# Moving the weight loads and weight casts of a fused convolution and token-mixer kernel onto the GpSimd queue, with a new job order

## The chip, the cores and the metric

The kernel runs on one core of a Trainium2 chip. The metric is the device time of one execution in microseconds (us), given as the median of several executions. "Span" is the time from the first to the last instruction of one profiled execution; the profiled execution of the kernel before took 160.67 us, 2.1 us longer than its span. Engines: TensorE (PE), VectorE (DVE), ScalarE (ACT), GpSimd (POOL), and the sync queue (SP), which only issues transfers.

## The reference

For each of 8 batches, x has 4224 rows of 192 columns. A causal convolution of 7 taps, one filter for each of 8 heads of 24 columns, gives y. Then a token mixer without a softmax follows:

```python
out = np.einsum('hk,bskhg->bshg', softmax(w), x_unf)      # y: 7-tap causal convolution
wq, wk = y @ w_q, y @ w_k                                 # 192 -> 64
W_tok = scale * np.einsum('bsd,btd->bst', wq, wk)
mixed = np.einsum('bst,btd->bsd', W_tok, y)
return np.maximum(mixed, 0.0) @ w_out
```

The kernel uses that mixed = wq (wk^T y) scale, and wk^T y = w_k^T (y^T y). So each batch needs y^T y once (the Gram matmuls), a small product M, and then Z = wq M, a ReLU and the output product.

## The kernel before

The convolution is a matmul with a band matrix (jobs Y); its result is evacuated to SBUF as `y`. The Gram matmuls (jobs G) want 64 of the 192 columns of y a second time beside the others, so a **duplicate copy** (job D, 128 x 1152 elements for half a batch) is made by DVE for batches 0 and 1 and by POOL for later ones. Then come Q (y with w_q), the small products for M, Z, and O (the output product). A small scheduler in the kernel file simulates all engines, gives each job a priority (`KEYS`), and so fixes each engine's instruction order at build time.

POOL issues the loads of x, which cast f32 to bf16 on the way (their queue, q0, counts 13.63 MB written, and the page has 27.73 MB read from HBM).

```python
    def load(b, part):                      # issued by POOL
        if b < NX and b not in zero:        # NX = 5 buffers for x
            zero[b] = [pool(lambda e: e.memset(XW[0:6, b, 0, 0, :], 0.0)),
                       pool(lambda e: e.memset(XW[:, b, :, NCK - 1, :], 0.0))]
        ...
        if part == 0:
            first(b, xg[b][0], old)                  # two small loads around the halo
            rows(b, 0, 1, 0, 128, 8, xg[b][0], old)
            rows(b, 1, 0, 0, 128, 9, xg[b][0], old)
        else:
            rows(b, 0, 9, 0, 128, 8, xg[b][1], old)
            rows(b, 1, 9, 0, 128, 8, xg[b][1], old)
            last(b, xg[b][1], old)
    ...
    for b in range(2, NX):                  # all ahead of the first duplicate
        load(b, 0)
        load(b, 1)
    ...
    def prefetch(b, part):                  # later loads, after a duplicate
        if b < B:
            load(b, part)
    ...
            if what == "dup":
                if key[1] > 1:              # batches 2 to 7
                    eng = "pool"
                    begin[eng] = max(free[eng], at)
    ...
        if kind == "D" and job.name[1] > 0:
            prefetch(job.name[1] + NX - 1, job.name[2])
```

The weights wk and wo come by the sync queue in f32, and ten small jobs on ACT and DVE cast them:

```python
        job_w("wk", 0, WK[:, 0], twice(WST[:, 0, 0:DH]), 128, 1),
        ...
        job_w("wo", 3, WO2S[:, :], WST[:, 3, :], D, 2),
```

Of the kernel before, what the change touches and what calls it, by code (L numbers as in the profile page):

```python
# [13 lines left out]
KEYS = {  # L14
    "E": -2.342, "Y": (-1.064, 1.033, 0.024), "Q": (-0.288, 1.999, -0.374), "G": (0.16, 0.5, 0.0),
    "Z": (0.931, 0.953, 0.0), "O": (1.4, 0.82, 0.0),
}

EDGES = {}


CLOCK = {
    "x0": (6.0, 8.2, 8.6, 9.8, 11.9, 13.7, 15.5, 16.5), "band": 6.7, "wq": 7.2, "wk": 15.0,
    "wo": 18.5, "now": 0.05, "hold": 1.5, "fill": 24.0, "issue": 3.0,
    "dma": (377e3, 14.5, 1.6, {"x": 3.0, "o": 1.2}),
# [138 lines left out]
def bass_lightweight_conv__then__hypermixer_token_mlp_kernel(  # L164
# [34 lines left out]
    def sbuf(name, shape, dtype):  # L199
# [18 lines left out]
    BANDL = sbuf("bandl", [128, H, 128], BF16)  # L218
    IDENT = sbuf("ident", [128, 128], BF16)
    WST = sbuf("wst", [128, 4, D], F32)  # L220
# [15 lines left out]
    WARM = sbuf("warm", [128, 128], BF16)  # L236
# [6 lines left out]
    THREES = ((0, 1, 2), (3, 4, 5), (6, 7))  # L243
    GROUPS = [[
        ((0,), 1, 6, FOURS), ((1,), 0, 5, FOURS), ((0,), 0, 1, (FOURS[0] + FOURS[1],)),
        ((0,), 6, 11, FOURS), ((1,), 5, 10, FOURS), ((0,), 11, 18, THREES), ((1,), 10, 14, FOURS),
        ((1,), 14, 18, FOURS),
    ]] + [[((0, 1), 0, 9, PAIRS), ((0, 1), 9, 18, PAIRS)]] * (B - 1)
# [46 lines left out]
    )  # L295
    for i in range(4):
        P.dma(
            "sp",
            lambda e, i=i: e.dma_start(
                WSQ[32 * i : 32 * i + 32, :, :].rearrange("p (m r) d -> p m (r d)", m=3),  # L300
                bass.AP(wq_t, 0, [[2 * DH, 32], [64 * DH, 3], [1, 2 * DH]]),
            ),
            wl[0],
        )
# [7 lines left out]
    z_m = dve(lambda e: e.memset(M_SB[:, :, :], 0.0))  # L312
    z_bandl = act(lambda e: e.memzero(BANDL[:, :, :]))  # L313
    z_ones = act(lambda e: e.activation(ONES[:, :], WARM[0:H, :], AF.Identity, bias=1.0), [z_warm])

    rows(0, 0, 1, 0, 128, 5, xg[0][0], ())
    bits = pool(lambda e: e.iota(BITS[:, :], [[1, H]], base=127, channel_multiplier=-1))
    rows(0, 1, 0, 0, 128, 5, xg[0][1], ())
    first(0, xg[0][2], z_first)
    rows(0, 0, 6, 0, 128, 5, xg[0][3], ())  # L320
# [7 lines left out]
    def wload(slot, p0, p1, src, row0, width, grp, deps, col=0):  # L328
        P.dma(
            "sp",  # L330
            lambda e: e.dma_start(
                WST[p0:p1, slot, col : col + width],
                bass.AP(src, row0 * width, [[width, p1 - p0], [1, width]]),
            ),
            grp, deps,
        )

    for s, (src, wd) in enumerate(((wk_t, DH), (wo_t, D))):
        wload(2 * s, 0, 128, src, 0, wd, wl[s + 1], [xg[0][2 * s]])
        if s == 0:  # L340
            wload(1, 0, 128, src, 64, wd, wl[1], ())
            wload(0, 0, 64, src, 128, wd, wl[1], (), DH)
            wload(0, 64, 128, src, 0, wd, wl[1], (), DH)
        else:
            wload(3, 0, 64, src, 128, wd, wl[2], ())
            wload(3, 64, 128, src, 128, wd, wl[2], ())


    def warm(n, deps):
        def f(e):  # L350
            for _ in range(n):
                o = e.matmul(PS[:, 0, 0:128], WARM[:, :], WARM[:, :], start=True, stop=True)
            return o

        return P.op("pe", f, deps)

    warm(16, [z_warm])
# [20 lines left out]
    zero = {}  # L378
    for b in range(1, NX):
        if b < 3:  # L380
            zero[b] = [act(lambda e, b=b: e.memzero(XW[0:6, b, 0, 0, :])),
                       act(lambda e, b=b: e.memzero(XW[:, b, :, NCK - 1, :]))]
    z_wk = act(lambda e: e.memzero(WK[:, 3:6]))
    z_wo2 = act(lambda e: e.memzero(WO2[:, :]))
# [37 lines left out]
    for q, eng in enumerate(("act", "dve", "act", "dve")):  # L422
# [3 lines left out]
        def f(e, q=q, x0=x0, x1=x1, s0=s0, eng=eng):  # L426
# [6 lines left out]
    wqs = [act(lambda e: e.copy(WQ[:, :, :], WSQ[:, :, :]), [wl[0]])]  # L433

    short = [dve(lambda e: e.tensor_copy(BANDL[0:64, :, 0:LAST], BAND[0:64, :, 0:LAST]),
                 [*band, z_bandl])]

    def load(b, part):
        if b < NX and b not in zero:
            zero[b] = [pool(lambda e: e.memset(XW[0:6, b, 0, 0, :], 0.0)),  # L440
                       pool(lambda e: e.memset(XW[:, b, :, NCK - 1, :], 0.0))]
        old = zero[b] if b < NX else [
            done[("Y", b - NX, g, k)] for g, q in enumerate(GROUPS[b - NX]) for k in range(len(q[3]))
        ]
        if part == 0:
            first(b, xg[b][0], old)
            rows(b, 0, 1, 0, 128, 8, xg[b][0], old)
            rows(b, 1, 0, 0, 128, 9, xg[b][0], old)
        else:
            rows(b, 0, 9, 0, 128, 8, xg[b][1], old)  # L450
            rows(b, 1, 9, 0, 128, 8, xg[b][1], old)
            last(b, xg[b][1], old)

    load(1, 0)
    load(1, 1)
    ident = pool(lambda e: e.memset(IDENT[:, :], 0.0))
# [6 lines left out]
    )  # L463
    z_zr = pool(lambda e: e.memset(ZR[:, :, 1, :], 0.0))
    for b in range(2, NX):
        load(b, 0)
        load(b, 1)
    warm(20, [])


    class Job:
        def __init__(self, name, key, banks, pe, cols, reads=(), after=(), evacs=(), then=None,
# [4 lines left out]
            self.pe_us = sum(max(n, 64) / 2400 + 0.0025 for n in cols)  # L477

    made = {"short": short, "band": band, "ident": [ident], "wq": wqs, "z_m": [z_m], "z_zr": [z_zr]}
# [13 lines left out]
    def parts(c0, c1):  # L493
        if c1 < NCK:
            return [(BAND, c0, c1)]
        return [(BAND, c0, c1 - 1), (BANDL, c1 - 1, c1)]

    def bands(c1):
        return ["band", "short"][: 1 + (c1 == NCK)]

    def job_y1(b, g, k):
# [3 lines left out]
        w = GRP * n  # L505

        def pe(e, bk):
            for j, h in enumerate(hs):
                for band_, a0, a1 in parts(c0, c1):
                    rhs = XW[:, b % NX, half, a0:a1, GRP * h : GRP * h + GRP]  # L510
                    o = PS[:, bk, w * j + GRP * (a0 - c0) : w * j + GRP * (a1 - c0)]
                    last = e.matmul(o, band_[:, h, :], rhs, start=True, stop=True,  # L512
                                    skip_group_check=True)
            return last

        def make(bk):
            o = bass.AP(
                Y, (b % 2) * NCK * 2 * YW + c0 * 2 * YW + YW * half + GRP * hs[0],
                [[2 * NCK * 2 * YW, 128], [GRP, len(hs)], [2 * YW, n], [1, GRP]],
            )  # L520
            i = PS[:, bk, 0 : w * len(hs)].rearrange("p (h c d) -> p h c d", c=n, d=GRP)
            return [(o, i)]

        return Job(
            ("Y", b, g, k), ykey(b, c0 + n * k / len(heads)), 1, pe,
            [GRP * (a1 - a0) for _, a0, a1 in parts(c0, c1)] * len(hs),
            reads=bands(c1), groups=[xg[b][g]],
# [3 lines left out]
    def job_y(b, g, hp):  # L531
# [5 lines left out]
        def pe(e, k):  # L537
            for j in range(2):
                h = 2 * hp + j
                for band_, a0, a1 in parts(c0, c1):  # L540
                    rhs = XW[:, b % NX, :, a0:a1, GRP * h : GRP * h + GRP]
                    o = PS[:, k + j, 48 * (a0 - c0) : 48 * (a1 - c0)]
                    last = e.matmul(  # L543
                        o.rearrange("p (c h d) -> p h c d", h=2, d=GRP), band_[:, h, :], rhs,
                        start=True, stop=True, skip_group_check=True,
                    )
            return last

        def make(k):
# [8 lines left out]
            ("Y", b, g, hp), ykey(b, c0 + n * hp / 4), 2, pe,  # L558
            [48 * (a1 - a0) for _, a0, a1 in parts(c0, c1)] * 2,
            reads=bands(c1), groups=[xg[b][g]],  # L560
            after=[("TD", b - 2, k) for k in range(6)] + [("G", b - 2, c) for c in range(NCK)],
            evacs=[(make, ("Y", b, g, hp), 96 * n, "copy")],
        )
# [68 lines left out]
    def job_g(b, c):  # L632
        def pe(e, bk):
            for h in range(2):
                y = Y[:, b % 2, c, h, :]
# [35 lines left out]
    def job_mm(b):  # L671
        def pe(e, bk):
# [10 lines left out]
            reads=[("wk", k) for k in range(6)] + ["z_m", ("GS", b), ("GT", b)],  # L683
# [56 lines left out]
    def job_o(b, i, q):  # L740
# [35 lines left out]
        def then():  # L776
# [21 lines left out]
            def landed(t, st=st):  # L798
                st.end = t

# [8 lines left out]
            reads=[("wo", k) for k in range(4)] + [("Z", b, i, k) for k in range(1 if rem else 3)],  # L809
# [4 lines left out]
    def twice(ap):  # L814
        return ap.unsqueeze(1).to_broadcast([ap.shape[0], 2, DH])

    def job_w(name, k, o, i, n, l, deps=()):
        return Job(
            ("W", name, k), KEYS["E"] + 0.01 * k, 0, None, [], reads=list(deps), groups=[wl[l]],
            evacs=[(lambda bk: [(o, i)], (name, k), n, "cast")],  # L820
        )

    made["z_wk"], made["z_wo2"] = [z_wk], [z_wo2]
    casts = [
        job_w("wk", 0, WK[:, 0], twice(WST[:, 0, 0:DH]), 128, 1),
        job_w("wk", 1, WK[:, 1], twice(WST[:, 1, 0:DH]), 128, 1),
        job_w("wk", 2, WK[:, 2], twice(WST[:, 0, DH : 2 * DH]), 128, 1),
        job_w("wk", 3, WK[0:64, 3], twice(WST[0:64, 0, 0:DH]), 128, 1, ["z_wk"]),
        job_w("wk", 4, WK[64:128, 4], twice(WST[64:128, 0, 0:DH]), 128, 1, ["z_wk"]),
        job_w("wk", 5, WK[64:128, 5], twice(WST[64:128, 1, 0:DH]), 128, 1, ["z_wk"]),  # L830
# [285 lines left out]
```

## Time and profile before

| | before |
|---|---|
| time, median of 3 | 161.17 us |
| span, granted clock | 158.6 us, 0.995 |
| busy PE, ACT, DVE, POOL | 91%, 81%, 74%, 39% |
| first output matmul | 31.21 us |
| end of the last matmul (its end is modelled) | 152.2 us |

### The profile page before, as it was taken

The page shows a single profiled execution, that of the slowest core. Times are in us where ns is not written, and L with a number is a line of the kernel's source. Part 1 is how long each engine was busy: PE and PEld are TensorE (multiplying, and loading weights), DVE is VectorE, ACT ScalarE, POOL GpSimd, SP SyncE. Part 2 cuts the span into 40 slices and gives each one's busy share as a digit, 9 for nine tenths or more (in the row PEclk, how much of TensorE's full clock was granted, in tenths as well). Part 3 has the DMA queues.
Part 4 walks back from the last instruction along what each step waited for, and adds up shares of the span by engine and source line. Part 5 has one row for each costly group of instructions (what it writes and reads, how often), then busy time and mean ns, then how long its engine had stood idle before and what let it go on. Part 6 is the DMA issues. An engine that isn't in the chain of part 4 may idle for free.

```text
span 158.6 us, 5869 instructions
## 1 busy us (share of the span) xinstructions
PE 144.7 (91%) x2553; PEld 110.3 (70%) x2584; DVE 117.3 (74%) x233; ACT 128.9 (81%) x225; POOL 62.0 (39%) x83
## 2 busy tenths in 40 slices
PE   5899968999998999999999999999999999999930
PEld 4899753777776667766776787687767777876720
DVE  6767757998748788869778887997679739556700
ACT  8633838999877999899799887978798989799960
POOL 7999999899990855022002020202011020000000
PEclk9999999999999999999999999999999999999997
DMA  2999999999999999999999999999996554679997
GB/s 44 187 179 205 191 191 192 191 190 268 213 258 310 300 200 283 330 256 298 288 296 286 297 290 243 278 336 295 251 346 235 199 207 189 236 269 371 360 386 256
DMA packets 48281, 40.44 MB, mean 255 GB/s; under 512 B 38144, under 2 KB 40320, under 8 KB 48256
## 3 DMA queue, kind: packets, MB, share of 16 engines
q0 software_dynamic: 36784, 13.63, 72.2%
q1 hardware_dynamic: 11472, 26.45, 46.2%
q8 instruction: 20, 0.33, 0.8%
q14 instruction: 5, 0.04, 0.1%
HBM read 27.73 MB, written 25.95 MB: 339 GB/s over the span
## 4 chain that ended last, share of the span: by engine, by line
PE 80%; ACT 8%; DVE 5%; issue 3%; ACTq 0%
PE ps L637 17%; PE ps L756 13%; PE ps L543 12%; PE ps L758 12%; PE ps L608 9%; PE ps L713 9%; ACT y L955 3%; PE ps L512 2%; PE ps L966 2%; ACT o_sb L955 1%; DVE yb L953 1%; PE ps L677 1%; DVE shift L415 1%; ACT L313 1%; ACT qt L955 1%
## 5 line engine op out<-in xcount | busy, mean ns | idle before, releaser
L955 ACT COPY o_sb<-ps 128x768 f32<-128x768 f32 (+1 forms) x63 | 47.2, 778 | 4.6 <-PE ps L758 3.4
L955 ACT CAST y<-ps 128x864 bf16<-128x864 f32 (+4 forms) x52 | 41.0, 814 | 6.7 <-PE ps L512 5.4
L756 PE MATMUL ps<-wo,zt 128*128 128x192 bf16 x256 | 42.6, 248 | 0.4 <-DVE m_sb L961 0.2
L758 PE MATMUL ps<-wo,zt 128*128 128x384 bf16 x128 | 41.7, 326 | 0.0
L268 POOL DMA_DIRECT2D xw<-in_x_dram x51 | 40.8, 820 | 1.5 <-POOLq L1101 0.8
L955 POOL COPY y<-y 128x1152 bf16<-128x1152 bf16 x12 | 13.9, 1155 | 66.6 <-ACT y L955 52.9
L637 PEld LDWEIGHTS ps<-y 128*128 128x128 bf16 x864 | 32.5, 98 | 8.5 <-ACT y L955 0.8
L637 PE MATMUL ps<-y 128*128 128x64 bf16 x864 | 35.8, 193 | 1.5 <-ACT y L955 0.4
L959 DVE TENSOR_SCALAR zt<-ps 128x512 bf16<-128x512 f32 x47 | 31.2, 683 | 7.8 <-PE ps L713 5.7
L953 DVE STREAM_TRANSPOSE yb<-y 128x576 int32<-128x576 int32 x48 | 33.6, 748 | 0.4 <-ACT y L955 0.2
L756 PEld LDWEIGHTS ps<-wo,zt 128*128 128x128 bf16 x256 | 25.6, 115 | 9.4 <-ACT o_sb L955 1.3
L543 PE MATMUL ps<-xw,band 128*128 128x432 bf16 (+1 forms) x112 | 28.5, 336 | 0.7 <-ACT m_sb L960 0.3
L958 ACT ACTIVATE zt<-ps 128x512 bf16<-128x512 f32 x49 | 28.8, 635 | 0.0
L955 DVE CAST y<-ps 128x864 bf16<-128x864 f32 (+2 forms) x20 | 19.3, 964 | 8.3 <-PE ps L543 5.4
L713 PE MATMUL ps<-qt,m_sb 128*128 128x512 bf16 x65 | 21.8, 380 | 0.3
L955 ACT CAST qt<-ps 128x576 bf16<-128x576 f32 (+2 forms) x21 | 11.7, 583 | 8.4 <-PE ps L608 8.4
L608 PE MATMUL ps<-yb,wq 32*64 32x288 bf16 x768 | 15.7, 284 | 0.9 <-issue 0.4
L955 DVE CAST qt<-ps 128x234 bf16<-128x234 f32 (+1 forms) x27 | 10.3, 419 | 8.2 <-PE ps L608 8.2
L543 PEld LDWEIGHTS ps<-xw,band 128*128 128x128 bf16 x112 | 9.8, 97 | 7.2 <-ACT m_sb L960 0.7
L758 PEld LDWEIGHTS ps<-wo,zt 128*128 128x128 bf16 x128 | 14.5, 113 | 0.0
L713 PEld LDWEIGHTS ps<-qt,m_sb 128*128 128x128 bf16 x96 | 8.8, 97 | 5.6 <-ACT y L955 0.9
L608 PEld LDWEIGHTS ps<-yb,wq 32*64 32x64 bf16 x768 | 10.5, 102 | 2.4 <-issue 1.3
(78 smaller groups left out, 118.9 us busy)
## 6 DMA issues: line engine op xcount, KB each, us to landing
out_dram<-o_sb SPq DMA_DIRECT2D x31, 768.0 KB, 7.3
xw<-in_x_dram POOLq DMA_DIRECT2D x21, 384.0 KB, 26.8
xw<-in_x_dram POOLq DMA_DIRECT2D x7, 432.0 KB, 26.1
xw<-in_x_dram POOLq DMA_DIRECT2D x4, 240.0 KB, 5.2
out_dram<-o_sb SPq DMA_DIRECT2D x16, 48.0 KB, 5.7
out_dram<-o_sb SPq DMA_DIRECT2D x2, 384.0 KB, 3.2
xw<-in_x_dram POOLq DMA_DIRECT2D x8, 42.0 KB, 13.4
xw<-in_x_dram POOLq DMA_DIRECT2D x1, 288.0 KB, 6.1
```

The lines of the kernel that those rows point to most:

```text
L268: return e.dma_start(XW[lo:hi, b % NX, half, c : c + n, :], bass.AP(x_t, at, [[D, hi - lo], [CW * D, n], [1, D]]),)
L512: last = e.matmul(o, band_[:, h, :], rhs, start=True, stop=True, skip_group_check=True)
L543: last = e.matmul(o.rearrange("p (c h d) -> p h c d", h=2, d=GRP), band_[:, h, :], rhs, start=True, stop=True, skip_group_check=True,)
L608: last = e.matmul(PS[64 * h : 64 * h + 64, bk + i, 0:288], WQ[r, j, :], rhs, start=j == 0, stop=j == 5, skip_group_check=True)
L637: last = e.matmul(PS[:, 7, 64 * k : 64 * k + 64], y[:, 64 * k : 64 * k + 128], y[:, 64 * k : 64 * k + 64], start=c + h + k == 0, stop=c == ...
L713: return e.matmul(PS[:, bk, :], m[:, parts[k] : parts[k] + 128], q, start=True, stop=True)
L756: e.matmul(o[:, 192 * h : 192 * h + 192], z[:, h, cols], WO1[:, :], start=h == 0, stop=False, **kw)
L758: last = e.matmul(o[:, 0:384], z[:, 2, cols], WO2[:, :], start=False, stop=True, **kw)
L953: return e.transpose(o, i)
L955: return e.copy(o, i) if eng == "act" else e.tensor_copy(o, i)
L958: return e.activation(o, i, AF.Relu)
L959: return e.tensor_scalar(o, i, 0.0, None, op0=ALU.max)
```

## The change

The intent was to shorten the start and to take small work off the busy engines. Batch 0's first two groups of x come by the sync queue in f32 and are cast on ACT and DVE; the halo rows of later batches are zeroed on DVE and not loaded apart; the last, short chunk uses the same band matrix; batch 0's band jobs may fill two PSUM banks; the weights are cast in their load, which POOL then issues; dummy matmuls that keep TensorE busy at the start are longer and fewer; the job priorities are new. The core of the diff:

```diff
-            first(b, xg[b][0], old)
-            rows(b, 0, 1, 0, 128, 8, xg[b][0], old)
-            rows(b, 1, 0, 0, 128, 9, xg[b][0], old)
+            for half in range(2):
+                rows(b, half, 9 * part, 0, 128, 9 - part, xg[b][part], old)
...
     load(1, 0)
+    wload(WK[:, 0], wk_t, 0, DH, wl[1], 2)            # on POOL, cast on the way
+    wload(WK[:, 1], wk_t, 64, DH, wl[1], 2)
+    wload(WK[0:64, 2], wk_t, 128, DH, wl[1], 2)
+    wload(WK[64:128, 2], wk_t, 0, DH, wl[1], 2)
+    wq = [pool(lambda e: e.tensor_copy(WQ[:, :, :], WSQ[:, :, :]), [wl[0]])]
     load(1, 1)
+    z_m = pool(...)      # and z_wk
+    load(1, 2)
+    wk = [pool(lambda e, o=o, i=i: e.tensor_copy(o, i), [wl[1]]) ...]     # 3 copies
+    load(1, 3)
+    wload(WO1[:, :], wo_t, 0, D, wl[2])               # and two more
+    load(2, 0)
+    z_wo2 = pool(...)
+    load(2, 1)
+    wo = [pool(lambda e, o=o, i=i: e.tensor_copy(o, i), [wl[2]]) ...]     # 2 copies
-    for b in range(2, NX):
+    for b in range(3, NX):
         load(b, 0)
         load(b, 1)
...
 KEYS = {
-    "E": -2.342, "Y": (-1.064, 1.033, 0.024), ...
+    "E": -4.9, "Y": (-1.039, 1.337, 0.0), ...         # new everywhere, and EDGES by batch
-                o = e.matmul(PS[:, k, 0:128], WARM[:, :], WARM[:, :], ...)
+                o = e.matmul(PS[:, k, 0:256], WARM[:, 0:128], WARM[:, 0:256], ...)
```

## The prediction

> **What bounds the kernel now.** I first read the engine shares of the page (TensorE 91% busy, the highest), then the chain of waits in order of time, then the busy time by stretch, then the DMA part.
>
> The chain gives the start-up and the real pace of TensorE, since its entries run from start to start:
>
> ```profile
> 6.59 0.98 PE ps L512 x8
> 7.57 1.39 PE ps L966 x13
> ...
> 9.97 0.81 PE ps L966 x12
> 10.99 0.87 PE ps L637 x30
> 12.08 0.56 PE ps L966 x10
> ...
> 19.69 0.35 ACT wo L955
> 20.04 0.25 ACT wo2s L955
> ...
> 21.60 1.03 issue
> 22.62 0.55 PE ps L966 x7
> ...
> 26.64 1.65 PE ps L713 x6
> 28.29 0.35 PE ps L637 x12
> ...
> 102.17 0.43 PE ps L713 x2
> ```
>
> Columns: start, length, what. The L966 pieces are dummy matmuls that only bridge idle time. L637 (the Gram jobs) takes 0.35/12 = 29 ns a matmul, L713 0.43/2 = 215 ns. The same view gives 90 ns per 216-column band matmul (0.36 for two of 432 columns), about 0.9 us per group of 48 in the Q job, and 0.33 us per output bank (0.17 for two of 192 columns, 0.16 for one of 384). Each is close to columns/2400 us + 2.7 ns. Over all jobs of the program that is 131 us of real TensorE work, without dummies. TensorE works from 6.59 to 152.0 us, so 14.5 us are lost, and they are not spread evenly:
> - up to the first output matmul (31.21 us in the timeline): 24.6 us hold 14.8 us of work. **9.8 us lost.**
> - from there to 152.0: 120.8 us hold 116.1 us. **4.7 us lost**, 4%.
> - after TensorE's end, 6.6 us of last evacuations and stores to the span's end at 158.6.
>
> So the start is worth attacking; the middle is nearly full. The stretches show the second resource (columns as in the page: the stretch, its length, busy time of PE, PEld, DVE, ACT, POOL, then granted clock, DMA share, GB/s):
>
> ```profile
> 24.00:34.00 10.00, 9.48 (x144) 6.13 (x146) 9.00 (x16) 9.81 (x16) 9.53 (x14) 1.00 1.60 192
> 60.00:80.00 20.00, 19.63 (x397) 14.78 (x409) 16.59 (x34) 18.02 (x30) 3.77 (x4) 1.00 1.28 295
> 120.00:130.00 10.00, 9.57 (x218) 7.65 (x221) 7.43 (x15) 8.91 (x18) 0.35 (x1) 1.00 0.56 213
> ```
> ```profile
> q0 software_dynamic: 36784, 13.63, 72.2%
> q1 hardware_dynamic: 11472, 26.45, 46.2%
> q8 instruction: 20, 0.33, 0.8%
> ```
>
> Queue q0 is the load of x, counted as written in bf16; in f32 it reads twice that, 27.3 MB. So 192 GB/s before the stores begin is 0.38 MB/us of reading, and 60 to 80 us (1.65 MB by q0, 4.2 by q1 in that window) is (3.3 + 4.2)/20 = 0.375 MB/us. Loads and stores together, 53 MB, need about 142 us of DMA: nearly the whole span. DMA has slack only after the last load landed (about 118 us, where q0 runs dry) and the share falls to 0.56. The DMA is a near second bound.
>
> [...]
>
> **The change part by part.**
> 1. *Input of batch 0.* Two of POOL's ten issues (820 ns each) move to the idle sync queue as plain f32 loads into unused output buffers, so the later groups are issued 1.6 us earlier. Before, TensorE still waits for the x DMA of group 6 at 16.3 us; the change's own timing table puts the last group at 13.7 instead of 16.5. Added: two casts of 128x960, one on ScalarE ahead of the band copies. From the 480- and 864-column casts (559, 903 ns) I estimate 1.0 us; if its data land by 4.8 us the band is not late by more than 0.2 us.
> 2. *Halo.* Per later batch two small loads go and one 6x96 memset comes (138 ns on DVE), saving 2 x 0.8 us of POOL issue, which is hidden after 40 us. Little.
> 3. *Last chunk.* The second band matrix goes: 72 band matmuls and 72 weight loads less, 0.8 us of TensorE, 0.45 of it after the first output. The Gram matmul contracts over 44 rows but streams as many columns: nothing.
> 4. *Two-bank jobs.* One 1.0 us evacuation for two of 0.56 and 0.66: about 0.2 us of evacuator time each, but 0.4 us more latency. Neutral.
> 5. *Weights cast in their load.* Ten small casts leave ScalarE and DVE between 15 and 21 us; the two lines of the chain above (0.60 us) and the cast at 16.23 (0.29) go. Added to POOL: 7 issues of about 0.7 us, and small copies, between the loads of batch 1. POOL is full until 34 us, but each issue of 9 chunks feeds 2.3 us of DMA.
> 6. *Dummies.* In the instruction order 83 fillers of 128 columns become 11 of 256, and 36 warm-up ones become 10 long ones. Filler on the chain is 1.39 + 0.81 + 0.56 + 0.55 = 3.3 us; now at most 1.2. [...]
> 7. *Order.* Job priorities are new everywhere; batch 1's band runs per half.
>
> Timeline of the new start, from those durations: bands until 10.4 us; 30 Gram matmuls to 11.3; the last group lands at 13.7, its band ends at 14.2; Q 15.6; 48 Gram 17.0; second Q after three transposes (0.75 us each) 18.2; the small products and eight batch-1 bands 19.1; then Z from about 19.8 (before: 26.64). The first output follows 5 us of work later, at about 25.4 (before 31.2), when the output weights must have landed too. From there 115.6 us of work and the same 4.7 us of losses end TensorE at 145.7; with [...] 1.0 us for late x (below), 146.4. The tail is as before: in both orders 8.2 us of output matmuls stand behind batch 7's last small products, and the last evacuations queue on ScalarE. Plus 6.6: span 153.0. Reported time minus span is 161.17 - 158.6 = 2.6, so about **155.5**; I put 155.0, as the new order was surely tuned for more than I can count.
>
> **The rivals.**
> - *x becomes the bound.* Stores start 6 us earlier and share the DMA. At 0.375 MB/us, 19 MB of x left at 27.5 us plus 15.5 MB of stores ahead of it put batch 7's second part at about 120 us; a PE that runs 6 us earlier would want it near 117, where before it had 6 us of slack. For it: DMA share never falls before 118. Against it: other work can be placed in between. Cost 0 to 4 us: 155 to 158. The halo memset would then also block DVE's queue while it waits for the load.
> - *POOL becomes the start-up bound.* With weight issues among the loads, batch 1 or the output weights land late; each us goes straight to the end: 156 to 158.
> - *Evacuation.* ACT is 81% busy, and 97% in the last windows. In a tighter middle it could bind: 1 to 2 us.
> - *The new order is better than mine.* If the middle lost 2 us instead of 4.7: 152.
>
> **Range and chances.** From 151.3 (full start gain, better middle) to 158.6 (x or POOL takes most back). Faster by over 2% means below 157.9: 0.80. Slower would need a stall of 9 us: 0.03.
>
> **What would show it.** Right: first output matmul at 24.5 to 27 us, L1016 fillers near 1 us, no weight casts on ACT and DVE, TensorE's end near 146, a tail of about 6.6. Wrong: first output after 29 (POOL, output weights), TensorE or DVE waiting for the x load after 90 us (DMA bound), or a DMA queue that is saturated to the end while TensorE idles.

The cuts marked in it took out what no trace or run of this case shows: a paragraph of general statements on matmul times, the supply of instructions and DMA issue; the last sentence of part 6, on what fewer instructions save; and in the timeline a term of 0.3 us for that. The sum is 25.4 + 115.6 + 4.7 = 145.7, less 0.3 us, plus 1.0 for late x: 146.4, and with the tail 153.0. The entry "issue" of 1.03 us in the chain is time in which the engine waits for nothing that the profile shows; its cause was not shown.

Some of its statements with their measured numbers: columns/2400 us + 2.7 ns is the fit to the readings named before it (29 ns for 64 columns and 215 for 512 are 0.415 ns a column); the Q job does not follow it (48 matmuls of 288 columns in 0.9 us, 19 ns each). The 142 us of DMA are an estimate, 53 MB at the 0.375 MB/us read from the trace. The 0.8 us of part 3 are an estimate: before, 432 columns took 0.188 us in two matmuls (four such pairs in 0.75 us from 29.03 us), after, 0.183 us in one (four in 0.73 us from 52.44 us), so 5 ns less each, 0.4 us if all 72 saved as much. The Gram matmul over 38 rows took 192 ns in the mean of the changed kernel, that over 128 rows 194. The 2.3 us of DMA for 9 chunks are about 0.88 MB read at 0.375 MB/us.

## More of the kernel before

In the page's rows by slice (a slice is 4 us, a digit is the busy share in tenths), POOL is full for the first 12 slices, about 47 us, partly busy to about 63 us, and nearly idle afterwards:

```profile
POOL 7999999899990855022002020202011020000000
PEclk9999999999999999999999999999999999999997
```

And POOL's timeline around 40 us (start, length, instruction; L268 and L284 are load issues, L955 is the duplicate copy of batch 2's first half):

```profile
34.23 4.82 POOL L268 DMA_DIRECT2D xw<-in_x_dram  x6
38.99 0.72 POOL L284 DMA_DIRECT2D xw<-in_x_dram  x1
39.67 1.20 POOL L955 COPY y<-y 128x1152 bf16<-128x1152 bf16 x1
```

The reader is to see that a load issue occupied POOL for most of a microsecond (51 issues at L268, 820 ns each in the mean), and that the first duplicate stands directly behind a run of them, at 39.67 us, in the midst of the full stretch. TensorE did not wait for it in this kernel: it had other work until then. So the average (POOL 39% busy) says nothing of this place.

The scheduler's own picture of POOL stayed: it assumes POOL free at 28.0 us, in both kernels.

## The result, and the profile after

The changed kernel is correct and took **167.33 us** (166.39 to 167.98, 4 runs) against 161.14 us of the kernel before on the same chip. The ratio of the fast runs is 1.040, 95% interval 1.032 to 1.047: **slower**. Here and below a ratio is the mean time of one kernel's fast runs over that of the kernel before in the same rounds, so it is not quite the ratio of the medians. Executions over 1.5% slower than the fastest of the same kernel are left out of the means.

| | before | after | predicted |
|---|---|---|---|
| span | 158.6 | 164.6 | 153.0 |
| first Z matmul | 26.64 | 21.83 | 19.8 |
| first output matmul | 31.21 | 27.97 | 25.4 |
| end of last matmul | 152.2 | 157.2 | 146.4 |
| first output to there | 121.0 | 129.2 | 121.0 |
| from there to the end | 6.4 | 7.4 | 6.6 |
| granted clock | 0.995 | 0.966 | |

The start did gain 3.2 us. The middle lost 8.2, the tail 1.0: together 6.0 us, the difference of the spans. The waits of TensorE name most of it (columns: who waits, for whom, us in total, times, longest):

```profile
PE ps L680 <- POOL y L989: 5.6, 1, 5.6
...
PE ps L546 <- DVE xw L989: 1.1, 1, 1.1
PE ps L799 <- POOL wo L500: 0.9, 1, 0.9
```

One wait of 5.6 us, for POOL's duplicate copy of batch 2. The chain of what ended last, which held PE at 80% and no POOL before, now runs over POOL (the page's shares, then its entries in order of time: start, length, what):

```profile
PE 62%; POOL 20%; ACT 6%; DMA 4%; issue 3%; ACTq 0%; POOLq 0%
```
```profile
10.53 7.09 DMA wk<-in_moe_w_k_dram
17.67 0.29 POOL wk L489
...
28.69 3.81 POOL xw L303 x4
32.49 0.67 POOL xw L319
...
34.05 3.79 POOL xw L303 x4
37.84 0.67 POOL xw L319
38.52 0.87 POOL xw L303
39.49 2.81 POOL xw L303 x3
42.31 0.67 POOL xw L319
43.02 1.15 POOL y L989
44.22 0.50 PE ps L680 x6
```

From 28.69 us on, these are the load issues of batches 3, 4 and 5, about 4.5 us a batch (the 35 issues at L303 took 937 ns each in the mean), and only then, at 43.02, the copy that TensorE needs. Its own inputs were ready at 39.64, when ACT finished the last evacuation it reads. In the kernel before the same copy ran at 39.67. Higher up in the chain stands the reason that POOL is late: it stood still for 1.29 us until wk had landed (17.67), because the wk copies are in its queue ahead of further loads; and there are seven more issues and six more copies in that queue, and three memsets (1.7 us together) that DVE and ACT did before. The copy comes 3.35 us later than before (43.02 against 39.67), and TensorE comes to it earlier.

The rows by slice show the same place, full until about 49 us on POOL (the duplicates stand inside this stretch), and a dip of the clock that the kernel before does not have:

```profile
POOL 7998698989990761110220200202020200000000
PEclk9999999999579999999999999999999999999995
```

The stretches show what the dip costs (columns: stretch, length, busy us of PE, PEld, DVE, ACT, POOL, then granted clock, DMA share, GB/s):

```profile
40.00:44.00 4.00, 0.00 (x0) 0.00 (x0) 1.23 (x2) 0.00 (x0) 3.95 (x5) 0.58 1.51 229
44.00:48.00 4.00, 3.78 (x39) 2.69 (x40) 0.25 (x1) 1.87 (x3) 4.00 (x5) 0.56 1.39 252
48.00:52.00 4.00, 4.00 (x113) 3.46 (x110) 1.94 (x4) 2.77 (x6) 1.66 (x3) 1.00 1.60 192
```

While TensorE was idle the granted clock fell to one half, and it stayed there after work had resumed: PE is "busy" from 44 to 48 us, but issues 39 matmuls where the next 4 us hold 113 (of other shapes). The 1-us stretches show 1.00 until 40 us, 0.83 at 40 to 41, 0.50 from 41 to 47, 0.75 at 47 to 48 and 1.00 from 48. By these means the clock fell about 2.0 us after the last matmul had ended at 38.6, and returned about 3.3 us after the first matmul at 44.22. I estimate from this that about 3.3 us at half speed cost some 1.6 us.

### The profile page after: what moved, and what is told of

It reads as the page before. It is cut to its first block, busy times and chain, and to the rows that moved or that the text cites. A ratio compares the mean times of both kernels' runs of the same rounds, so it can differ in the third digit from the quotient of the medians.

```text
span 164.6 us, 5582 instructions
## 1 busy us (share of the span) xinstructions
PE 145.4 (88%) x2430; PEld 103.4 (63%) x2430; DVE 111.8 (68%) x211; ACT 130.2 (79%) x235; POOL 61.1 (37%) x82
## 4 chain that ended last, share of the span: by engine, by line
PE 62%; POOL 20%; ACT 6%; DMA 4%; issue 3%; ACTq 0%; POOLq 0%
POOL xw L303 13%; PE ps L680 12%; PE ps L799 11%; PE ps L580 10%; PE ps L801 10%; PE ps L756 10%; PE ps L650 6%; DMA wk<-in_moe_w_k_dram 4%; ACT o_sb L989 4%; POOL xw L319 2%; ACT zt L992 1%; POOL wk L373 1%; POOL xw L458 1%; POOL y L989 1%; PE ps L720 1%
## 5 line engine op out<-in xcount | busy, mean ns | idle before, releaser
L989 ACT COPY o_sb<-ps 128x768 f32<-128x768 f32 (+1 forms) x61 | 45.5, 787 | 3.6 <-PE ps L801 2.9
L989 ACT CAST y<-ps 128x864 bf16<-128x864 f32 (+6 forms) x48 | 38.6, 852 | 10.9 <-PE ps L580 6.7
L680 PEld LDWEIGHTS ps<-y 128*128 128x128 bf16 (+1 forms) x864 | 33.2, 98 | 15.6 <-POOL y L989 6.0
L680 PE MATMUL ps<-y 128*128 128x64 bf16 (+1 forms) x864 | 36.6, 194 | 6.2 <-POOL y L989 5.6
L799 PEld LDWEIGHTS ps<-wo,zt 128*128 128x128 bf16 x256 | 26.5, 116 | 11.3 <-ACT o_sb L989 1.8
L303 POOL DMA_DIRECT2D xw<-in_x_dram x35 | 32.3, 937 | 2.0 <-POOL xw L458 1.1
L756 PE MATMUL ps<-qt,m_sb 128*128 128x512 bf16 x96 | 28.5, 380 | 0.5 <-DVE m_sb L995 0.3
L992 ACT ACTIVATE zt<-ps 128x512 bf16<-128x512 f32 x49 | 27.7, 620 | 0.3 <-PE ps L756 0.3
L989 DVE CAST y<-ps 128x864 bf16<-128x864 f32 (+3 forms) x20 | 19.8, 992 | 8.5 <-PE ps L580 6.4
L580 PE MATMUL ps<-xw,band 128*128 128x432 bf16 x96 | 24.8, 356 | 0.0
L989 DVE COPY o_sb<-ps 128x768 f32<-128x768 f32 (+1 forms) x11 | 7.4, 675 | 8.0 <-PE ps L794 6.7
```

The costliest lines, as they stand in the source:

```text
L303: return e.dma_start(XW[lo:hi, b % NX, half, c : c + n, :], bass.AP(x_t, at, [[D, hi - lo], [CW * D, n], [1, D]]),)
L580: last = e.matmul(PS[:, k + j, 0 : 48 * n].rearrange("p (c h d) -> p h c d", h=2, d=GRP), BAND[:, h, :], rhs, start=True, stop=True,)
L680: last = e.matmul(PS[:, 7, 64 * k : 64 * k + 64], y[:, 64 * k : 64 * k + 128], y[:, 64 * k : 64 * k + 64], start=c + h + k == 0, stop=c == ...
L756: return e.matmul(PS[:, bk, :], m[:, parts[k] : parts[k] + 128], q, start=True, stop=True)
L799: e.matmul(o[:, 192 * h : 192 * h + 192], z[:, h, cols], WO1[:, :], start=h == 0, stop=False, **kw)
L989: return e.copy(o, i) if eng == "act" else e.tensor_copy(o, i)
```

## The experiments

The theory (**P**): POOL's in-order queue. The change put weight issues and small copies into it, so the load issues of batches 3 to 5 end later, the duplicate of batch 2 stands behind them, and TensorE, which now comes to this point earlier, waits 5.6 us and then runs at half clock. Rivals: **D**, the load of x has become the bound, and any order that favours the copies will only wait for x; **O**, the new job order is bad in itself. Sixteen kernels ran, all correct. Unless I say otherwise, "after" is the changed kernel and each edit is made to it. They ran with the kernel before beside them, at a median of 161.44 us for e1, e5, e2 and e4; 161.53 for e11, e12, e3 and e7; 161.52 for e6, e13, e14 and e15; 162.49 for e16 and e17; 161.61 for e18 and e19 (of all its executions, slow ones too). The medians of the kernel before differ by up to 1.3 us (161.14 to 162.49).

### Only POOL's order: one duplicate first (e1)

The first duplicate of batch 2 goes ahead of the issues of batch 5. The orders of all other engines are identical: in the traces of e1 and e5 the 2430, 235 and 211 instructions of PE, ACT and DVE come in the same order as in the changed kernel's.

```diff
+        if job.name == ("D", 2, 0):
+            load(5, 0); load(5, 1)        # were ahead of it
```

> One part moved: on POOL alone, the copy of batch 2's first half (the 128x1152 duplicate in y) stands before the five load issues of batch 5 instead of behind them; every other engine's order is unchanged. Theory P (the loss is POOL's in-order queue: TensorE idles 5.6 us for that copy, and then runs about 4 us at half clock): the copy ends near 39.7 instead of 44.2 us, but the copy of the second half stays behind the loads (at 46 us), so the wait should move there and shrink to about 3 us; time 163 to 165 us, against 167.3 for the changed kernel. Rival D (the load of x is the bound, the wait only covers it): no gain, 167. Rival O (the new order of jobs is worse throughout): no gain, 167.

Measured: 164.11 us (1.014, 1.006 to 1.021), 3.2 us less than after. The first copy cost 1.13 us of waiting, and the longest wait, 2.8 us, moved to the second copy, which now stood behind the loads of batch 5; the clock stayed at 1.00 in every 1-us stretch from 38 to 50 us:

```profile
PE ps L680 <- POOL y L989: 3.9, 2, 2.8
```

### Only POOL's order: both duplicates first (e5)

```diff
+        if job.name == ("D", 2, 1):
+            load(5, 0); load(5, 1); load(6, 0)
```

> On POOL alone, both copies of batch 2 stand before the load issues of batch 5 and of the first half of batch 6; all other engines unchanged. Theory P: TensorE's wait near 38 to 44 us goes to about 1 us or less, the granted clock stays 1.00 in 40 to 48 us, time 159.5 to 162 us. Rival D: delaying those loads makes x later, TensorE waits for the x load further on, time 167 or more. Rival O: at most 1 us of gain, 166 to 167.

Measured: **160.79 us** (0.993, 0.987 to 0.9995), 6.5 us less than after, from an exchange of a few instructions on one engine that is 37% busy. POOL's timeline now reads (start, length, instruction):

```profile
38.84 1.14 POOL L989 COPY y<-y 128x1152 bf16<-128x1152 bf16 x1
40.47 1.14 POOL L989 COPY y<-y 128x1152 bf16<-128x1152 bf16 x1 [0.50 <-POOL y L989]
41.56 3.79 POOL L303 DMA_DIRECT2D xw<-in_x_dram  x4
```

The copies run at 38.84 and 40.47, the waits fall to 1.6 us, the clock is 0.991. The loads of batches 5 and 6 went out later by up to 3 us, and TensorE waited for none of them: D is rejected for this order. P holds for the loss of 6 us.

### The wait kept, but filled (e2)

Fifty dummy matmuls of 256 columns run before the Gram matmul that waits; POOL's copy stays where it was.

```diff
+        if job.name == ("G", 2, 0):
+            fill(k, 50, banks[k][1])
```

> The wait stays, but 50 dummy matmuls of 256 columns (about 5.4 us) are put on TensorE right before the waiting Gram matmul. Separates the wait from the clock that it costs. If the half clock after the wait costs what the stretch shows (about 1.5 us of work missing in 44 to 48 us), the clock stays 1.00, TensorE still resumes at 44.2 us, and the time falls by 1 to 2 us, to 165.3 to 166.3. If the clock drop is only a mark in the record, no change: 167.3.

Measured: 165.44 us (1.024). The copy still ran at 43.15, but the clock did not fall:

```profile
40.00:44.00 4.00, 4.00 (x39) 3.52 (x36) 1.36 (x3) 0.00 (x0) 3.95 (x5) 1.00 1.53 224
44.00:48.00 4.00, 3.85 (x108) 3.06 (x106) 1.21 (x2) 2.36 (x3) 4.00 (x5) 1.00 1.38 258
```

So the half clock after the wait costs time of its own: 1.9 us by the medians (167.33 - 165.44), 1.05 us between the two profiled executions (166.39 and 165.34). In the traces the first Q job behind the wait starts 1.4 us earlier (47.24 against 48.66), which is in keeping with the 1.6 that I had worked out; at the last matmul 0.6 us of it is left (156.56 against 157.18).

### The weights off POOL (e4)

The weights come again by the sync queue in f32 and are cast by ten copies on ACT and DVE, at fixed places; TensorE's order is identical, POOL loses seven issues and five copies.

```diff
-    wload(WK[:, 0], wk_t, 0, DH, wl[1], 2)                    # POOL, and six more
+    wload(0, 0, 128, wk_t, 0, DH, wl[1])                      # sync queue, f32, and six more
+    # ten casts on act / dve after the band jobs of batch 0 and after its Gram
```

> One part undone: the weights are loaded in f32 by the sync queue and cast by ScalarE and DVE (as before the change), with the same job order on every engine. It takes seven DMA issues, five copies and a wait of 1.3 us off POOL, about 7 us before 30 us. Theory P: both copies of batch 2 come about 6 to 7 us earlier, TensorE no longer waits for POOL, the first output matmul comes at 26.5 to 27.5 instead of 28.0; time 158.5 to 161 us. Rival D: no gain. Rival O: at most 1 us of gain.

Measured: **160.18 us** (0.991, 0.983 to 0.998). No wait for POOL is left in its list, and the first duplicate now waits for its own input, not for the queue:

```profile
37.85 1.14 POOL L1013 COPY y<-y 128x1152 bf16<-128x1152 bf16 x1 [1.38 <-ACT y L1013]
```

So undoing this one part of the change undoes the loss, without touching the order of loads and duplicates. It paid at the start: TensorE waited 1.9 us for x before 14 us, and its first output came at 29.0, where I had expected 26.5 to 27.5. That the early f32 weight loads took the DMA from x is my reading; e16 below, which holds them back, has 0.3 us of this wait.

### A lean POOL queue (e11)

Zeroing moved to ACT, output weights issued and copied earlier, both duplicates first; PE's and DVE's orders identical.

```diff
+    z_wk = act(lambda e: e.memzero(WK[:, 3:6]))      # and z_wo2, and three tail memsets
-    z_wk = pool(...)
+    wload(WO1[:, :], ...)                            # right behind wk
```

> The changed kernel with its weights still cast in their load on POOL, but POOL relieved: the zeroing of the three x tails and of two weight tiles goes to ScalarE's idle start, the output weights are issued right behind the key weights, and both copies of batch 2 stand before the later x loads. Orders of TensorE and DVE unchanged. Theory P: POOL is 3 to 4 us ahead of where it was, no wait of TensorE on POOL above 0.5 us, first output matmul at 27.0 to 27.5 us; time 157.5 to 160.5 us, a little under the run where only the copies were moved (160.8). If what is left beyond POOL is the order itself, it stays at 160 to 161.

Measured: 160.07 us (0.993, 0.986 to 0.999), with POOL's duplicates at 37.10 and 40.34. One wait for them is left, 1.0 us where I expected at most 0.5, and the first output came at 28.30, not at 27.0 to 27.5. Good for 7.3 us against after, and no better than e4 or e5. Something else holds at 160.

### The scheduler told when POOL is free (e12)

```diff
-    ... "dve": CLOCK["band"], "pool": 28.0}
+    ... "dve": CLOCK["band"], "pool": 38.5}
```

> The changed kernel with one number altered: the scheduler inside the program assumes that POOL is free for its first copy at 38.5 us (what the trace shows) instead of 28.0. POOL's own order stays; TensorE's order is the same up to the matmul that waited, and then takes other work. Theory P (root cause: the order was laid for a POOL that is 10 us ahead of the real one): the wait of 5.6 us falls below 2 us, the clock stays at 1.00, time 158.5 to 162 us. If the wait can't be filled because no other work is ready, the time stays above 164.

A miss: 166.89 us (1.034). The wait for POOL's copy went and the clock was 0.995, but the new job order has other waits (x 1.6, the halo memset 1.3, POOL's output weights 1.2, an output buffer 1.1 us). By its time it falls in the branch in which TensorE finds no other work, but the reason of that branch does not hold: other work was found, and the loss came elsewhere. The cause of each new wait was not tested.

### The old job order (e3)

The whole change, but with the priorities of the kernel before.

```diff
-KEYS, EDGES of the change
+KEYS, EDGES of the kernel before, B = (0, 0)
```

> The new priorities of the jobs undone (those of the kernel before put back, output hold-back off), all the rest of the change kept. Rival O (the new order is what costs): 160 us or less. Theory P: POOL is as late as ever (its own order is unchanged, copy of batch 2 at about 43 us) and the old priorities reach the same Gram jobs at a similar point, so TensorE still waits 3 to 6 us for POOL; time 164 to 168 us.

Measured: 169.74 us (1.053). It waits 4.0 us for POOL's copy and 2.8 for POOL's output weights. It is slower than I had expected (164 to 168). The old order does not mend it, and e5 removes the loss with the new order kept, so O is rejected as the cause.

### The kernel before with the weights on POOL (e7)

The opposite test: of all parts only this one, put into the kernel before.

```diff
     load(1, 0)
+    wload(WK[:, 0], ...)           # POOL, cast on the way
+    wk = [pool(...)]               # waits for wk's landing
     load(1, 1)
```

> One part of the change alone on the kernel before: the weights cast in their load, issued by POOL, with the memsets and copies that this brings to POOL; the ten casts leave ScalarE and DVE. Theory P: POOL's first copy of batch 2 moves from 39.7 to about 47 us, TensorE waits 3 to 6 us for it, time 163.5 to 167 us, slower than before. Rival: the part is harmless by itself: 160 to 161.5 us.

Measured: 177.44 us (median of three fast runs; 1.101). The direction is as expected, the size far over it, and that is my own placing: POOL stood 5.4 us for wk's landing before it went on to batch 1's loads and the identity matrix.

```profile
PE ps L639 <- POOL y L947: 7.5, 1, 7.5
PE ps L665 <- POOL ident L450: 6.1, 1, 6.1
```

It shows the mechanism in a kernel without any other part of the change: a copy that waited 5.4 us for its DMA, in the queue that issues the loads, delayed what stood behind it (6.1 us of TensorE's waiting for the identity matrix, 7.5 us for the duplicate).

### Both remedies together (e6), and with the old order (e13)

e6 is e4 plus e5. e13 is e6 with the old priorities.

```diff
 # e6: the diffs of e4 and e5
 # e13: these, and the diff of e3
```

> The changed kernel with both reliefs of POOL at once: weights by the sync queue in f32, cast on ScalarE and DVE (as in e4), and both duplicate copies of batch 2 ahead of the loads of batch 5 and of the first half of batch 6 (as in e5). PE's instruction order is that of the changed kernel. If POOL's queue is all that the change lost by, and the two reliefs add up: no POOL wait, but e4 alone already had none, so the second relief should add nothing: 159.5 to 160.7 (e4: 160.2). If what keeps these versions at 160 is still POOL (late loads, late copies), it would come to 158 or less. If the loads of batch 5, now later, are missed: above 161, with a wait of PE for the x load.

> As e6, but with the job priorities of the kernel before. It asks what the new job order is worth once POOL holds nothing up. If the new order was the gain that I credited to it: e13 is slower than e6, by 2 us or more (162 and above). If the order is neutral: within 1 us of e6. If the new order itself is what costs the middle and the tail (PE's end minus first output 122 to 123 us against 120.8 before, tail 7.4 against 6.6): e13 comes to 157 to 158.5, with a tail near 6.6.

Measured: e6 160.62 us (1.001, 0.987 to 1.015), e13 164.36 us (1.021, 1.014 to 1.028). The remedies do not add up. Under equal conditions the new order is worth 3.7 us over the old by the medians (3.3 by the means; one of e6's runs took 162.53), so the credit that I gave it was right in kind.

### The duplicates on DVE (e14, e15)

e14 gives batch 2's duplicates to DVE; the scheduler knows it, and the order of the later jobs moves. e15 has e11's lean queue as well.

```diff
-                if key[1] > 1:
+                if key[1] > 2:
                     eng = "pool"
```

> The changed kernel with one condition changed: the two duplicate copies of batch 2 go to DVE (as those of batches 0 and 1 do) instead of to POOL; the scheduler knows it, so the order of the jobs after it moves somewhat. If the wait for POOL's queue is the cause: no wait of PE for POOL's copy near 40 us, clock above 0.98, 159 to 162. If the work on DVE takes what POOL's wait gave back (DVE as the new bound in 30 to 50 us): 162 to 165 with waits of PE on DVE there. If neither matters: 167.

> e11's early output weights and zeroing on ScalarE, together with e14's duplicates of batch 2 on DVE, and the loads in their own order again. A try for a version that beats both kernels. First output matmul at about 27.3 (no wait for POOL's output-weight copies). If start and middle are both free of POOL: 157.5 to 160. If the middle and the tail are the bound and the start doesn't reach the end: 160 as in e5, e4 and e11.

Measured: e14 165.17 us (three fast runs; 1.025; the profiled execution was slow, 168.13), e15 163.40 us (three fast runs; 1.017). Both miss. POOL's wait is gone, and TensorE waits for x instead, in e14 5.0 us for one load near 123 us (in that slow execution), in e15 2.0 us in two waits:

```profile
PE ps L580 <- DMA xw<-in_x_dram: 2.0, 2, 1.3
```

So D is a real second bound: it appears when the order uses x earlier. The load behind e15's longer wait landed at 100.7 us; the same load landed at 100.4 in e11, where nobody waited for it. None of these three changes of the scheduler's knowledge (e12, e14, e15) reached 160, while five kernels with TensorE's order untouched did (e4, e5, e6, e11, and e19 below came to 160 to 161; e18 to 161.25). That the priorities fit only the durations they were tuned with is my inference.

### The weights held back (e16)

Why did e4 and e5 stop at 160? Theory **P2**: POOL still sets the pace (the copy for batch 3 ran at 50.4 us in e5, e6 and e11), and e4 lost its start to its weight loads. Rival **L**: the later part is a limit by itself, and no better start reaches the end. e16 is e4 with the weight loads held until groups of x have landed.

```diff
-    wload(0, 0, 128, wk_t, 0, DH, wl[1])
+    wload(0, 0, 128, wk_t, 0, DH, wl[1], deps=[xg[0][5]])      # wo: xg[0][7]
```

> e4 with one thing changed: the f32 weight loads on the sync queue wait until the sixth (weights of the small products) and the eighth (output weights) load group of batch 0's x has landed, as the kernel before held them back. TensorE's order is that of the changed kernel. P2: TensorE's waits for x before 14 us go (1.9 to below 0.5), first Z matmul at about 22 instead of 23.9, first output at 27 to 28 instead of 29.0, last matmul 1 to 2 us earlier than e4's 151.6, time 158 to 159.2. L: the start is earlier, and the last matmul stays at 151.6, time 160 to 160.5. If the weights now land late (a wait of TensorE for their casts), 160 or above with first output after 28.5.

Measured: 164.14 us (1.013). The waits for x at the start went (0.3 us), but now the weights land late, and their casts stand in ACT's and DVE's queues ahead of copies that TensorE needs:

```profile
PE ps L681 <- DVE y L1013: 4.5, 1, 4.5
```

It is the same fault on other engines: a copy that waits for its DMA at the head of a queue. The half clock followed it too: TensorE idled from 16.3 us and was at work again from 20.8, and the clock was 0.85 in 19 to 20 us and 0.50 from 20 to 26. First output at 33.27, where the hoped-for branch had 27 to 28, and from there to the last matmul 122.6 us, exactly e4's figure.

### POOL's queue interleaved (e17), with the loads in order (e18)

Weights on POOL as in after. The small output-weight copies one load earlier, and the duplicates of batches 2 and 3 between loads; in the diff, (4, 1) is the load of batch 4's second half, and ("D", 2, 0) the duplicate of batch 2's first half, behind which it is issued. In e17 batch 7's first half slipped ahead of (6,1); e18 mends that.

```diff
+    after_dup = {("D", 2, 0): [(4, 1)], ("D", 2, 1): [(5, 0), (5, 1)],
+                 ("D", 3, 0): [(6, 0)], ("D", 3, 1): [(6, 1)]}        # e18: [(6, 1), (7, 0)]
```

> The changed kernel with POOL's instructions alone reordered, weights still cast in their load on POOL: the small output-weight copies one load earlier; batch 2's first duplicate copy before the second half of batch 4's load, its second copy before batch 5's loads, batch 3's copies before the two halves of batch 6. P2: no TensorE wait for POOL's copies above 0.5 us, first output at about 27.2 to 27.8, last matmul at 150 to 151, time 158 to 159.5. L: waits gone, last matmul at 151.6 and time 160 to 160.8 as e5. If the loads held back are missed (TensorE waiting for x after 60 us): above 161.

> e17 with all loads in their own order: batch 7's first half after batch 6's second. P2: first output at about 26.8 as in e17, no wait for x above 1 us, no wait for POOL's copies above 0.5, last matmul at 150 to 150.6 (26.8 + 123.5), time 158 to 159. L: last matmul at 151.6 although the first output comes 1.5 us earlier than in e5, time 160 to 160.8. If x is the second bound: TensorE waits for x after 95 us, and the time is above 160.

Measured: e17 167.0 and 169.0 us in its two fast runs (1.038). The profile is of a slow one (171.31); a single wait stands out in it:

```profile
PE ps L582 <- DMA xw<-in_x_dram: 10.1, 1, 10.1
```

So one half batch of x out of order is a wait of 10 us there, and by the fast runs 6.8 us of time against e18 (168.0 against 161.2): the loads have little slack. e18: 161.25 us (three fast runs, 161.13 to 161.33; three slow ones took 163.7 to 164.1; ratio 0.998, 0.991 to 1.004). Its first output is at 26.75 us, 1.5 us ahead of e5, and no wait for POOL's copies is in its list, yet its last matmul ends at 152.5. **P2 falls**: with POOL out of the way other waits take its place, among them one for x at 102.8 us, the branch of x as the second bound:

```profile
PE ps L682 <- issue: 2.7, 4, 0.9
...
PE ps L582 <- DMA xw<-in_x_dram: 1.1, 1, 1.1
```

"Issue" is time in which TensorE waits for nothing that the profile shows. The kernel before has two such waits in its list, 1.0 and 0.4 us. What causes them was not shown.

### The start alone (e19)

e5 with only the output-weight copies one load earlier.

```diff
-    load(2, 1)
     wo = [pool(...)]               # two copies
+    load(2, 1)
```

> e5 with the small output-weight copies one load earlier on POOL, nothing else. First output at about 27 instead of 28.26. P2 (POOL's first duplicate copy at 38.8 sets the pace until 40): the wait for it grows by about what the start gains, last matmul still at 151.6 to 152, time 160 to 161 as e5. If TensorE's own pace were all that matters after the first output: last matmul 1.2 us earlier, time 159.5.

Measured: 161.01 us (0.997, 0.992 to 1.001). The first output comes at 26.61 and the last matmul ends at 151.75, where e5 had 28.26 and 151.90: a start better by 1.65 us brings 0.15. The time is as P2 and L expected; the way there is only partly P2's. The wait for POOL's copies grew by 0.3 us (1.6 to 1.9), that for issue from 0.5 to 1.3 at the same Gram line.

| run | first output | last matmul ends | between | time |
|---|---|---|---|---|
| before | 31.21 | 152.2 | 121.0 | 161.1 to 162.5 |
| after | 27.97 | 157.2 | 129.2 | 167.33 |
| e5 | 28.26 | 151.9 | 123.6 | 160.79 |
| e4 | 29.00 | 151.6 | 122.6 | 160.18 |
| e11 | 28.30 | 151.7 | 123.4 | 160.07 |
| e6 | 28.42 | 151.8 | 123.4 | 160.62 |
| e18 | 26.75 | 152.5 | 125.8 | 161.25 |
| e19 | 26.61 | 151.8 | 125.1 | 161.01 |
| e16 | 33.27 | 155.9 | 122.6 | 164.14 |

All rows but the first have TensorE's order of the change. A start before 29 us does not reach the end; a later one (e16) does, in full. None of the versions beats both kernels by 2%; e4, e5 and e11 beat the kernel before by 0.7 to 0.9% by the ratios, with intervals that end just below 1. In e4 and e5 this rests in part on two executions of the kernel before at a lower clock (163.05 and 162.78 us, clock 0.98) that count as fast; against its other five (mean 161.28) e4 is 0.6% and e5 0.3% faster.

## Why the prediction was wrong

**The step that failed** is in part 5: "Added to POOL: 7 issues of about 0.7 us, and small copies, between the loads of batch 1. POOL is full until 34 us, but each issue of 9 chunks feeds 2.3 us of DMA." That looks at POOL as the feeder of the DMA alone. It has a second role, the duplicates, and these stand behind the issues in one queue. The sentence says that POOL is full until 34 us; the page's row has it full to about 47 (the stretch that the prediction shows ends at 34). What stands in that queue, and when TensorE wants it, was not asked. The answer was in the trace of the kernel before: the first duplicate at 39.67, with no gap ahead of it. What was added to POOL before that point delayed the copy (by 3.35 us, to 43.02), and what the start gained brought TensorE to it earlier (the first output by 3.2 us). e5, e4 and e1 show it by taking the wait away, e7 by making it in the kernel before.

**The rival "POOL becomes the start-up bound"** named the right engine and priced it at 156 to 158 us. It thought of late loads and late output weights only. The latter came, at 0.9 us. The main cost was the duplicate: 5.6 us of wait, and 1 to 2 us of half clock behind it, which no part of the prediction held (e2).

**The start.** Predicted first output 25.4, measured 27.97. (The prediction's own steps, 19.8 and 5 us of work, make 24.8; the 0.6 more has no source.) The mechanism was right, the size was off by 2.6 us, in several small terms: the bands of batch 0's last group ended at about 14.7 instead of 14.2; 48 Gram matmuls took 1.93 us instead of 1.4; 0.8 us of waits stand around the small products; and 0.9 us is the wait for the output weights. The part "Input of batch 0" was harmless but brought little: TensorE waited 1.1 us for the cast on DVE (9.08 us), and the 30 Gram matmuls began at 10.74, against 10.83 before.

**The middle.** "115.6 us of work and the same 4.7 us of losses", with 0.7 added (1.0 for late x, less 0.3): this term was 129.2 - 121.0 = 8.2 us too small. With the wait repaired it is still 1.6 to 2.6 us too small (between 122.6 and 123.6 against 121.0). That the losses are a constant that can be carried over from one order to another was the second wrong assumption. e19 shows it: a start 1.65 us earlier is lost again in the middle. Where exactly was not settled. The waits by name are POOL's copies, issue, and in e18 x; the rest is in waits too short for the list.

**The tail** was 7.4 instead of 6.6 us. It was 7.0 to 7.8 us in the ten other versions with TensorE's order of the change, 5.7 to 5.8 in the three runs with the old priorities (e3, e13, e7) and 6.4 in the kernel before. So it seems to go with the new order; no run tests that alone.

**x as the bound** did not occur in the changed kernel, but it was close: e14, e15, e17 and e18 all met it. The prediction read the last load's landing in the kernel before as about 118 us; the trace has 121.6, so there was less slack than it thought. Its estimate of about 120 for the changed kernel is met by e5 (120.2), in which TensorE doesn't stand still for the copy; in the changed kernel itself, which does, it was 115.1. A slip without effect: the last chunk's Gram matmuls contract over 38 rows in the trace, not 44; their mean, 192 ns against 194, bears out that this brings nothing. The new order was credited rightly (e6 against e13: 3.7 us). The sum: 2.6 (start) + 8.2 (middle) + 0.8 (tail) = 11.6 us, the difference between the predicted span of 153.0 and the 164.6 measured. The predicted time then adds 2.6 us for what lies outside the span, the median time less the span of another execution; in the profiled executions it is 2.1 before and 1.8 after. Without the POOL queue's part the change would have been a gain of 0.3 to 0.9% (e4, e5), not a loss of 4%.

## What to carry to other kernels

When work moves to an engine with a low average load, look at its queue in the order of time, up to the first instruction on which another engine waits. About 4.5 us of load issues ahead of the copy delayed it by 4.2 (it ran at 43.02 behind batch 5's issues, at 38.84 ahead of them in e5), and a copy that waited for its own DMA (1.29 us in the changed kernel, 5.4 in e7) held up what followed it. A gain at the start counted only up to the next limit (in e19, 1.65 us of it brought 0.15), so before adding it to the end, look for what the earlier engine will meet: here a copy queue, then waits of the kind "issue", then x. And an idle gap of 5.6 us on TensorE cost more than its length, by 1.05 to 1.9 us (e2), while in one of 2.8 us (e1) the clock stayed at 1.00.
